# Spectral mixer block with a gated MLP: the first 512 tokens dealt out anew, so that an x tile is one transfer

## The chip, the cores and the metric

One core of one Trainium2 chip runs the whole program. The metric is the device time of one execution in microseconds (us); the median of several runs is given with the lowest and the highest. Beside the times there is one execution recorded by the hardware profiler. In its rows PE is TensorE's matmuls and PEld its weight loads, DVE is VectorE, ACT ScalarE, POOL GpSimd and SP SyncE, which only issues transfers (DMA); a name with a q behind it (SPq, ACTq) is the engine's instruction queue. L190 is line 190 of the kernel.

## The reference

x is 2048 tokens by 512 channels in float32. Cut to what matters here:

```
h = layernorm(x) * (1 + ca) + sa                       # over the channels of each token
a = h @ dft_hid_re.T ;  b = h @ dft_hid_im.T           # 512 x 512
y = dft_seq_re @ a - dft_seq_im @ b                    # 2048 x 2048, over the tokens
x = x + ga * y
h = layernorm(x) * (1 + cb) + sb
z = gelu(h @ w_in) ;  z1, z2 = halves of z ;  z2 = layernorm(z2)
out = x + gb * ((z1 * (w_sp @ z2 + b_sp)) @ w_out)     # w_sp 2048 x 2048
```

sa, ca, ga, sb, cb and gb are six rows made from a conditioning vector c. The change touches only the first sum over tokens, dft_seq times the normed x.

## The kernel before

The kernel sums over tokens first: for each output quarter t (512 rows of the DFT), for the real and the imaginary matrix j, TensorE adds up 16 products, one for each tile s of 128 tokens: the normed tile (128 tokens by 512 channels, four weight blocks of 128 channels) by T, 128 tokens by 512 DFT rows. To keep float32's precision, each operand is split into a high part (rounded to the matmul's type) and a low part (the rest), and three matmuls stand for one (`matmul3`, lines 97 to 99).

The DFT matrices lie with the output row first, so a block must be turned before it can be multiplied. A stage is 512 DFT rows by 512 tokens (`quad`), loaded by `load_block` or, in halves of 64 columns, by `load_half`: partition 32a + j holds, for 16 values of b, the row 32b + j, at 128 columns of the a-th quarter. DVE turns 32 x 32 squares (`squares`, line 190): piece k of a stage gives T with partition 32a + i holding token 128a + 32k + i. The x tile that goes with it must have the same token in the same partition, so `load_x` and `load_two` load 32 partitions at a time, four transfers for a tile or group of tiles.

The order on each engine is written by hand. The start, at the end of the function body, deals with tiles 0 to 3 (g = 0) one by one: `load_two(0)` and `load_two(1)` put each tile's four transfers on the queues of SP and ACT, two each; `load_half` brings the first half of stage 0 in between, on both queues; tiles 2 and 3, the second half of stage 0, stage 1 and tiles 4 and 5 follow on SP. `keep_busy` lets TensorE multiply ones in the meantime. `stats_first` makes a tile's statistics on DVE with two small steps on GpSimd; `whole_first` norms tile 0 on ACT, unsplit; `hi_first`, `norm_x` and `lo_h` make the high and the low part (hh, hl) of tiles 1 to 3. `turn_whole` turns the first DFT piece unsplit; `prep_hi(n)` turns piece n on DVE and makes its high part AH on ACT, `prep_lo(n)` its low part AL on DVE. The engines take these in the order of the calls: DVE's is the statistics of tile 0, pieces 0 and 1, the statistics of tile 1, AL1, the statistics of 2 and 3, hl1, pieces 2 and 3, and so on. `mm_a(n)` is TensorE's share of piece n. For n = 0 it multiplies in plain float32 (line 543, two records for each matmul), for n = 1 to 3 it takes the three products one after the other for four channel blocks (line 549), and from n = 4 on it calls `matmul3`. Its four channel blocks go in the order 1, 2, 3, 0 for n below 4.

Of the 32 stages of DFT blocks, those with g = 0 hold the first 512 tokens: stages 0 and 1 in the first quarter, then one in four.

Of the kernel before, what the change touches and what calls it, by code (L numbers as in the profile page):

```python
# [20 lines left out]
def fnet_gmlp_kernel(  # L21
# [111 lines left out]
    def quad(a, r, k):  # L133
        return a[r * Q:(r + 1) * Q, k * Q:(k + 1) * Q]

    src = []
    for t in range(NQ):
        for g, j in ([(g, j) for g in range(NQ) for j in range(2)] if t == 0 else
                     [(g, j) for j in range(2) for g in range(NQ)]):
            src.append(quad((cr, ci)[j], t, g))  # L140
    N2 = 4 * len(src)
    N1 = N2 + 8
    YPROD = (6, 7, 4, 5, 3)
# [13 lines left out]
    def load_half(tile_, a, h, engs=(nc.sync,) * 4):  # L157

        v = a.rearrange("(b j) (a s) -> a j b s", j=32, a=4)
        for q in range(4):  # L160
            engs[q].dma_start(tile_[32 * q:32 * q + 32], v[q][:, :, 64 * h:64 * h + 64])

    XB = []

    def load(b):
        if b < len(src):
            stage[b] = blocks.tile([P, 16, P], F32, tag="stage", bufs=2, name=f"stage{b}")
            load_block(stage[b], src[b])
        elif b < len(src) + 2:
            j = b - len(src)  # L170
            XB.append(blocks.tile([P, 4, Q], F32, tag="stage", bufs=2, name=f"xb{j}"))
            for g in range(2):
                nc.sync.dma_start(XB[j][:, 2 * g:2 * g + 2], ht_d[g].rearrange("(k p) t -> p k t", p=P)[:, 2 * j:2 * j + 2])
                for kk in range(2):
                    TT[2 * j + kk, g] = XB[j][:, 2 * g + kk]
        elif 4 * (b - NB0) < NE - N4:
            i, gh = divmod(b - NB0, NQ)
            g, h = divmod(gh, 2)
            p = PROD[i]
            stage[b] = blocks.tile([P, 2, 16, 64], F32, tag="stage", bufs=2, name=f"stage{b}")  # L180
            for r in range(2):
                load_half(stage[b][:, r], s_d[S_OF[p], r, g] if p in S_OF else
                          quad(w_sp, r + (2 if p == 4 else 0), g + (2 if p == 1 else 0)), h)
# [68 lines left out]
    def prep_hi(n):  # L252
        if n >= NE or n in highs:
            return
        highs.add(n)
        if N2 <= n < N4:
            T[n] = form_t(n)
        else:
            b, k = divmod(n, 4) if n < N2 else (NB0 + (n - N4) // 4, (n - N4) % 4)
            if b != NB0:  # L260
                T[n] = blocks.tile([P, Q], F32, tag="t", bufs=2, name=f"t{n}")
            if b == NB0:
                assert n in T
            elif n >= N4:
                squares(T[n], stage[b][:, k % 2], k // 2)
            else:
                squares(T[n], stage[b], k)
        AH[n] = SE[2][:, n - N4] if N4 <= n < N4 + 4 else blocks.tile([P, Q], F32R, tag="ah", bufs=4, name=f"ah{n}")
        nc.scalar.activation(AH[n], T[n], AF.Copy)  # L269
        if not N2 <= n < N4 and k == 3:  # L270
            stage.pop(b)
            if b != NB0:
                load(b + 2)
# [91 lines left out]
    def keep_busy(n, k):  # L365

        ps = bank(k, "busyp")
        for _ in range(n):
            nc.tensor.matmul(ps, ones, busy, start=True, stop=True)

    def fold_sum(t, w, u):

# [49 lines left out]
    def load_x(g, ks=range(4), eng=nc.sync):  # L422
# [1 line left out]
        if g not in XG:  # L424
            XG[g] = spool.tile([P, 4, D], F32, tag="x", bufs=2, name=f"x{g}")
        k0, k1 = ks[0], ks[-1] + 1
        v = x.rearrange("(g a k i) d -> g a i k d", g=NQ, a=4, i=32)
        for a in range(4):
            eng.dma_start(XG[g][32 * a:32 * a + 32, k0:k1, :], v[g, a][:, k0:k1, :])
        for k in ks:  # L430
            X[4 * g + k] = XG[g][:, k, :]

# [12 lines left out]
        eng.tensor_scalar(mv[:, 3:4], mv[:, 0:1], mv[:, 2:3], -1.0, op0=ALU.mult, op1=ALU.mult)  # L445
        NRM[s] = mv[:, 2:3], mv[:, 3:4]

    two = (nc.sync, nc.sync, nc.scalar, nc.scalar)

    def load_two(k):  # L450
        if not k:
            XG[0] = spool.tile([P, 4, D], F32, tag="x", bufs=2, name="x0")
        v = x.rearrange("(g a k i) d -> g a i k d", g=NQ, a=4, i=32)
        for a in range(4):
            two[a].dma_start(XG[0][32 * a:32 * a + 32, k, :], v[0, a][:, k, :])
        X[k] = XG[0][:, k, :]

    def whole_first(s):

        LN[s] = spool.tile([P, D], F32, tag="xn", bufs=4, name=f"xn{s}")  # L460
        nc.scalar.activation(LN[s].rearrange("p (k a i) -> p k a i", a=4, i=32),
                             X[s].rearrange("p (a k i) -> p k a i", a=4, i=32), AF.Identity,
                             bias=NRM[s][1], scale=NRM[s][0])
        nc.scalar.activation(LN[s][:, :1], ones[:, :1], AF.Copy)

    def split_first(s):
# [6 lines left out]

    def turn_whole(n):
        T[n] = blocks.tile([P, Q], F32, tag="t", bufs=2, name=f"t{n}")
        squares(T[n], stage[0], n)
        highs.add(n)
        lows.add(n)

# [604 lines left out]
            mm([n])  # L1084


    load_two(0)
    stage[0] = blocks.tile([P, 16, P], F32, tag="stage", bufs=2, name="stage0")
    load_half(stage[0][:, :, :64], src[0], 0, two)
    load_two(1)  # L1090
    nc.scalar.activation(sc, ones[:, :ND], AF.Silu)
    load_x(0, range(2, 4))
    load_half(stage[0][:, :, 64:], src[0], 1)
    load(1)
    load_x(1, range(2))
    keep_busy(3, 5)
    ones_x(1)
    ones_x(2)
    ones_x(3)
    stats_first(0)  # L1100
    whole_first(0)
    turn_whole(0)
    prep_hi(1)
    stats_first(1)
    prep_lo(1)
    hi_first(1)
    stats_first(2)
# [342 lines left out]
```

## Time and profile before

| | us |
|---|---|
| median of 3 runs | 931.57 |
| lowest and highest | 931.29, 931.63 |
| the profiled execution's own time | 931.77 |
| its span, first to last instruction | 930.0 |

The page of the profile gives the busy time of each engine as a share of the span; that of TensorE tells nothing of single waits, which the list of waits does (who waited for whom, and how long in all). The chain of waits follows the work that ended last back from the end; the timeline lists an engine's instructions in order of time, runs of one kind merged (x4). Times count from the first instruction.

### The profile page before, as it was taken

The numbers are of one execution on the slowest core, as the hardware profiler recorded it, in microseconds if no ns is written. First come the engines' busy times: TensorE is split into PE (matmuls) and PEld (weight loads), VectorE is DVE, ScalarE is ACT, GpSimd is POOL, SyncE is SP. The second block draws the span as 40 slices with busy tenths as digits, with TensorE's granted clock in tenths as the row PEclk, the third lists the DMA queues.
The fourth block names the chain that finished last, engine by engine and source line by source line (L and its number), as shares of the span: only waits on it lengthen the run. The fifth ranks groups of instructions, "written<-read, shape, count | busy, mean of one in ns | idle before, by whom it ended". The sixth has DMA issues, their size and how long they took to land.

```text
span 930.0 us, 12339 instructions
## 1 busy us (share of the span) xinstructions
PE 924.2 (99%) x4053; PEld 760.4 (82%) x4053; DVE 738.2 (79%) x1218; ACT 409.1 (44%) x733; POOL 199.1 (21%) x375
## 2 busy tenths in 40 slices
PE   9999999999999999999999999999999999999998
PEld 5888888888888888888888888888888888888887
DVE  7799968787687677875678788899799789986762
ACT  5694424232132222322577877674544544331121
POOL 2330000224554165323512321331000000000000
PEclk9999999999999999999999999999999999999999
DMA  9995762856639977996463864444464566734651
GB/s 218 225 227 118 142 158 46 193 147 171 158 91 319 283 220 217 275 343 227 141 217 130 279 201 103 118 105 105 105 146 102 130 142 143 178 97 149 185 178 57
DMA packets 246976, 157.88 MB, mean 170 GB/s; under 512 B 140384, under 2 KB 214368, under 8 KB 246784
## 3 DMA queue, kind: packets, MB, share of 16 engines
q1 hardware_dynamic: 233248, 119.57, 52.2%
q0 software_dynamic: 12272, 36.86, 11.4%
q8 instruction: 32, 0.52, 0.2%
q10 hardware_dynamic: 1392, 0.66, 0.2%
q14 instruction: 32, 0.26, 0.1%
HBM read 120.33 MB, written 36.71 MB: 169 GB/s over the span
## 4 chain that ended last, share of the span: by engine, by line
PE 98%; DMA 1%; SPq 0%; ACTq 0%; DVE 0%; ACT 0%; issue 0%; DVEq 0%
PE gp L99 12%; PE gp L97 12%; PE gp L98 12%; PE gw L99 10%; PE gw L97 10%; PE gw L98 10%; PE yp L99 3%; PE yp L98 3%; PE yp L97 3%; PE op L98 3%; PE op L97 3%; PE op L99 3%; PE fp L98 1%; PE fp L97 1%; PE fp L99 1%; PE z2s L98 1%
## 5 line engine op out<-in xcount | busy, mean ns | idle before, releaser
L269 ACT ACTIVATE ah<-t 128x512 fp32r<-128x512 f32 x235 | 148.5, 632 | 362.6 <-DVE t L190 242.7
L287 DVE TENSOR_TENSOR al<-t,ah 128x512 fp32r<-128x512 f32 x235 | 160.6, 683 | 55.7 <-PE gp L98 30.9
L98 PE MATMUL gp<-al,hh 128*128 128x512 f32 x496 | 193.0, 389 | 0.0
L97 PE MATMUL gp<-ah,hh 128*128 128x512 f32 x496 | 193.0, 389 | 0.0
L99 PE MATMUL gp<-ah,hl 128*128 128x512 f32 x496 | 193.0, 389 | 0.0
L190 DVE STREAM_TRANSPOSE t<-stage 128x512 f32<-128x512 f32 x236 | 165.5, 702 | 6.3 <-DMA stage<-in_A_dft_seq_re_dram 3.1
L98 PE MATMUL gw<-al,bh 128*128 128x512 f32 x400 | 155.6, 389 | 0.0
L99 PE MATMUL gw<-ah,bl 128*128 128x512 f32 x384 | 149.5, 389 | 0.0
L97 PE MATMUL gw<-ah,bh 128*128 128x512 f32 x384 | 149.4, 389 | 0.0
L98 PEld LDWEIGHTS gp<-al,hh 128*128 128x128 f32 x496 | 93.1, 188 | 19.5 <-DVE al L287 0.2
L97 PEld LDWEIGHTS gp<-ah,hh 128*128 128x128 f32 x496 | 93.1, 188 | 19.4
L99 PEld LDWEIGHTS gp<-ah,hl 128*128 128x128 f32 x496 | 93.1, 188 | 19.3
L98 PEld LDWEIGHTS gw<-al,bh 128*128 128x128 f32 x400 | 75.1, 188 | 15.7
L99 PEld LDWEIGHTS gw<-ah,bl 128*128 128x128 f32 x384 | 72.1, 188 | 15.3 <-DVE bl L948 0.3
L97 PEld LDWEIGHTS gw<-ah,bh 128*128 128x128 f32 x384 | 72.1, 188 | 14.9
L920 POOL DMA_DIRECT2D s_d<-sj x64 | 35.1, 548 | 107.2 <-DVE sj L912 82.3
L97 PE MATMUL yp<-hth,gh 128*128 128x512 f32 x128 | 49.8, 389 | 0.0
L98 PE MATMUL yp<-htl,gh 128*128 128x512 f32 x128 | 49.8, 389 | 0.0
L99 PE MATMUL yp<-hth,gl 128*128 128x512 f32 x128 | 49.8, 389 | 0.0
L665 POOL DMA_DIRECT2D ht_d<-hturn x62 | 41.0, 667 | 23.1 <-DVE hturn L661 18.2
L97 PE MATMUL op<-woh,uh 128*128 128x512 f32 x110 | 42.8, 389 | 0.0
L98 PE MATMUL op<-wol,uh 128*128 128x512 f32 x110 | 42.8, 389 | 0.0
(247 smaller groups left out, 1449.4 us busy)
## 6 DMA issues: line engine op xcount, KB each, us to landing
stage<-in_A_dft_seq_im_dram SPq DMA_DIRECT2D x64, 256.0 KB, 6.0
sj<-in_B_w_sp_dram SPq DMA_DIRECT2D x32, 512.0 KB, 7.2
s_d<-sj POOLq DMA_DIRECT2D x64, 256.0 KB, 4.7
stage<-s_d SPq DMA_DIRECT2D x128, 128.0 KB, 2.9
stage<-in_A_dft_seq_re_dram SPq DMA_DIRECT2D x60, 256.0 KB, 5.6
stage<-in_B_w_sp_dram SPq DMA_DIRECT2D x88, 128.0 KB, 3.0
wm<-in_w_mod_dram SPq DMA_DIRECT2D x16, 256.0 KB, 6.1
xr<-in_A_x_dram POOLq DMA_DIRECT2D x16, 256.0 KB, 4.5
```

Source lines behind the costliest of these rows:

```text
L97: nc.tensor.matmul(acc, ah, bh, start=first, stop=False, skip_group_check=go_on)
L98: nc.tensor.matmul(acc, ah, bl, start=False, stop=False, skip_group_check=go_on)
L99: nc.tensor.matmul(acc, al, bh, start=False, stop=last, skip_group_check=go_on)
L190: nc.vector.transpose(dst.rearrange("p (b i) -> p b i", i=32), block[:, :, 32 * k:32 * k + 32])
L269: nc.scalar.activation(AH[n], T[n], AF.Copy)
L287: nc.vector.tensor_tensor(AL[n], t, AH[n].bitcast(F32), op=ALU.subtract)
L665: eng.dma_start(v[a, i], ht[32 * a:32 * a + 32].rearrange("c (b r) -> c b r", r=32))
L920: nc.gpsimd.dma_start(s_d[m, r, g][b * P:(b + 1) * P, :], a)
```

## The change

The first 512 tokens (g = 0) are dealt out anew: tile 2h + k holds in partition p the token 256h + 2p + k. A tile is then 128 rows of x at a distance of two rows, and `load_x` brings it in one transfer on SP; the tiles of the other three groups are loaded as before. To match, a stage with g = 0 is loaded by `load_pairs` in two halves of four transfers each (partition 32a + j takes columns 256h + 64a to 256h + 64a + 63), in pieces of 64 numbers (256 bytes), where `load_block` loads pieces of 128; and `turn_dft` turns it from every second column. ACT's queue keeps two transfers at the start, those of stage 0's first half. The normed tile 0 is made in two ACT steps of two channel blocks each (1 and 2, then 0 and 3). `keep_busy` issues two matmuls of 512 columns and one of 256 where it issued three of 512. The statistics of tile 1 go ahead of `prep_hi(1)`.

```diff
--- before.py
+++ after.py
@@ -133,11 +133,12 @@
     def quad(a, r, k):
         return a[r * Q:(r + 1) * Q, k * Q:(k + 1) * Q]
 
-    src = []
+    src, SRC_G = [], []
     for t in range(NQ):
         for g, j in ([(g, j) for g in range(NQ) for j in range(2)] if t == 0 else
                      [(g, j) for j in range(2) for g in range(NQ)]):
             src.append(quad((cr, ci)[j], t, g))
+            SRC_G.append(g)
     N2 = 4 * len(src)
     N1 = N2 + 8
     YPROD = (6, 7, 4, 5, 3)
@@ -160,12 +161,30 @@
         for q in range(4):
             engs[q].dma_start(tile_[32 * q:32 * q + 32], v[q][:, :, 64 * h:64 * h + 64])
 
+    def load_pairs(tile_, a, h, engs=(nc.sync,) * 4):
+
+        v = a.rearrange("(b j) (h a s) -> h a j b s", j=32, a=4, h=2)
+        for q in range(4):
+            engs[q].dma_start(tile_[32 * q:32 * q + 32, :, 64 * h:64 * h + 64], v[h, q])
+
+    def turn_dft(n, block, k):
+
+        if SRC_G[n // 4]:
+            squares(T[n], block, k)
+        else:
+            v = block.rearrange("p b (h i c) -> p b h i c", h=2, c=2)
+            nc.vector.transpose(T[n].rearrange("p (b i) -> p b i", i=32), v[:, :, k // 2, :, k % 2])
+
     XB = []
 
     def load(b):
         if b < len(src):
             stage[b] = blocks.tile([P, 16, P], F32, tag="stage", bufs=2, name=f"stage{b}")
-            load_block(stage[b], src[b])
+            if SRC_G[b]:
+                load_block(stage[b], src[b])
+            else:
+                for h in range(2):
+                    load_pairs(stage[b], src[b], h)
         elif b < len(src) + 2:
             j = b - len(src)
             XB.append(blocks.tile([P, 4, Q], F32, tag="stage", bufs=2, name=f"xb{j}"))
@@ -264,7 +283,7 @@
             elif n >= N4:
                 squares(T[n], stage[b][:, k % 2], k // 2)
             else:
-                squares(T[n], stage[b], k)
+                turn_dft(n, stage[b], k)
         AH[n] = SE[2][:, n - N4] if N4 <= n < N4 + 4 else blocks.tile([P, Q], F32R, tag="ah", bufs=4, name=f"ah{n}")
         nc.scalar.activation(AH[n], T[n], AF.Copy)
         if not N2 <= n < N4 and k == 3:
@@ -365,8 +384,8 @@
     def keep_busy(n, k):
 
         ps = bank(k, "busyp")
-        for _ in range(n):
-            nc.tensor.matmul(ps, ones, busy, start=True, stop=True)
+        for w in n:
+            nc.tensor.matmul(ps[:, :w], ones, busy[:, :w], start=True, stop=True)
 
     def fold_sum(t, w, u):
 
@@ -424,9 +443,14 @@
         if g not in XG:
             XG[g] = spool.tile([P, 4, D], F32, tag="x", bufs=2, name=f"x{g}")
         k0, k1 = ks[0], ks[-1] + 1
-        v = x.rearrange("(g a k i) d -> g a i k d", g=NQ, a=4, i=32)
-        for a in range(4):
-            eng.dma_start(XG[g][32 * a:32 * a + 32, k0:k1, :], v[g, a][:, k0:k1, :])
+        if g:
+            v = x.rearrange("(g a k i) d -> g a i k d", g=NQ, a=4, i=32)
+            for a in range(4):
+                eng.dma_start(XG[g][32 * a:32 * a + 32, k0:k1, :], v[g, a][:, k0:k1, :])
+        else:
+            v = x.rearrange("(g h p k) d -> g h p k d", g=NQ, h=2, k=2)
+            for k in ks:
+                eng.dma_start(XG[g][:, k, :], v[0, k // 2][:, k % 2, :])
         for k in ks:
             X[4 * g + k] = XG[g][:, k, :]
 
@@ -445,22 +469,16 @@
         eng.tensor_scalar(mv[:, 3:4], mv[:, 0:1], mv[:, 2:3], -1.0, op0=ALU.mult, op1=ALU.mult)
         NRM[s] = mv[:, 2:3], mv[:, 3:4]
 
-    two = (nc.sync, nc.sync, nc.scalar, nc.scalar)
-
-    def load_two(k):
-        if not k:
-            XG[0] = spool.tile([P, 4, D], F32, tag="x", bufs=2, name="x0")
-        v = x.rearrange("(g a k i) d -> g a i k d", g=NQ, a=4, i=32)
-        for a in range(4):
-            two[a].dma_start(XG[0][32 * a:32 * a + 32, k, :], v[0, a][:, k, :])
-        X[k] = XG[0][:, k, :]
+    def halves(h, s):
+
+        v = X[s].rearrange("p (a k i) -> p k a i", a=4, i=32)
+        for ks in (slice(1, 3), slice(0, 4, 3)):
+            nc.scalar.activation(h[:, ks], v[:, ks], AF.Identity, bias=NRM[s][1], scale=NRM[s][0])
 
     def whole_first(s):
 
         LN[s] = spool.tile([P, D], F32, tag="xn", bufs=4, name=f"xn{s}")
-        nc.scalar.activation(LN[s].rearrange("p (k a i) -> p k a i", a=4, i=32),
-                             X[s].rearrange("p (a k i) -> p k a i", a=4, i=32), AF.Identity,
-                             bias=NRM[s][1], scale=NRM[s][0])
+        halves(LN[s].rearrange("p (k a i) -> p k a i", a=4, i=32), s)
         nc.scalar.activation(LN[s][:, :1], ones[:, :1], AF.Copy)
 
     def split_first(s):
@@ -473,7 +491,7 @@
 
     def turn_whole(n):
         T[n] = blocks.tile([P, Q], F32, tag="t", bufs=2, name=f"t{n}")
-        squares(T[n], stage[0], n)
+        turn_dft(n, stage[0], n)
         highs.add(n)
         lows.add(n)
 
@@ -1084,24 +1102,24 @@
             mm([n])
 
 
-    load_two(0)
+    load_x(0, range(1))
     stage[0] = blocks.tile([P, 16, P], F32, tag="stage", bufs=2, name="stage0")
-    load_half(stage[0][:, :, :64], src[0], 0, two)
-    load_two(1)
+    load_pairs(stage[0], src[0], 0, (nc.sync, nc.sync, nc.scalar, nc.scalar))
+    load_x(0, range(1, 2))
     nc.scalar.activation(sc, ones[:, :ND], AF.Silu)
     load_x(0, range(2, 4))
-    load_half(stage[0][:, :, 64:], src[0], 1)
+    load_pairs(stage[0], src[0], 1)
     load(1)
     load_x(1, range(2))
-    keep_busy(3, 5)
+    keep_busy((Q, Q, Q // 2), 5)
     ones_x(1)
     ones_x(2)
     ones_x(3)
     stats_first(0)
     whole_first(0)
     turn_whole(0)
+    stats_first(1)
     prep_hi(1)
-    stats_first(1)
     prep_lo(1)
     hi_first(1)
     stats_first(2)
```

## Rows read from the trace of the kernel before

**Rows 1.** Page, busy times: us (share of the span) x instructions

```profile
PE 924.2 (99%) x4053; PEld 760.4 (82%) x4053; DVE 738.2 (79%) x1218; ACT 409.1 (44%) x733; POOL 199.1 (21%) x375
```

**Rows 2.** Waits of TensorE, whole run: us, times, longest us

```profile
PE gp L549 <- ACT ah L269: 0.7, 1, 0.7
```

**Rows 3.** Chain of waits, 0 to 16 us: start us, us, what

```profile
8.40 4.31 DMA stage<-in_A_dft_seq_re_dram
...
12.83 0.72 DVE t L190
...
13.57 0.64 ACT ah L269
```

**Rows 4.** Timeline of TensorE, 0 to 21 us: start, us, instruction, count, idle before

```profile
1.53 5.46 PE L369 MATMUL busyp<-busy,ones 128*128 128x512 f32 x6 [1.53 <-DVE busy L308]
6.82 3.85 PE L543 MATMUL gp<-t,xn 128*128 128x512 f32 x8
10.52 1.19 PE L549 MATMUL gp<-ah,hh 128*128 128x512 f32 x4
...
14.26 1.20 PE L549 MATMUL gp<-ah,hh 128*128 128x512 f32 x4 [0.72 <-ACT ah L269]
...
20.08 0.39 PE L98 MATMUL gp<-al,hh 128*128 128x512 f32 x1
```

**Rows 5.** DMA issues near 1 and 10.5 us: KB, us to landing

```profile
x<-in_A_x_dram ACTq DMA_DIRECT2D x2, 64.0 KB, 2.3
...
stage<-in_A_dft_seq_im_dram SPq DMA_DIRECT2D x2, 256.0 KB, 6.3
```

**Rows 6.** Timeline of DVE, 0 to 21 us

```profile
3.84 0.69 DVE L439 BATCH_NORM_STATS2 first<-x 128x6 f32<-128x512 f32 x1 [2.46 <-DMA x<-in_A_x_dram]
...
5.68 0.21 DVE L445 TENSOR_SCALAR first<-first 128x1 f32<-128x1 f32 x1 [0.74 <-POOL first L443]
5.96 1.30 DVE L190 STREAM_TRANSPOSE t<-stage 128x512 f32<-128x512 f32 x2
...
9.31 0.69 DVE L439 BATCH_NORM_STATS2 first<-x 128x6 f32<-128x512 f32 x1 [0.47 <-DMA x<-in_A_x_dram]
...
11.45 0.69 DVE L525 TENSOR_TENSOR hl<-xn,hh 128x512 fp32r<-128x512 f32 x1
...
17.72 1.30 DVE L190 STREAM_TRANSPOSE t<-stage 128x512 f32<-128x512 f32 x2
19.13 0.69 DVE L287 TENSOR_TENSOR al<-t,ah 128x512 fp32r<-128x512 f32 x1
```

**Rows 7.** Timeline of ACT, 0 to 21 us

```profile
5.93 0.81 ACT L461 ACTIVATE xn<-x,first 128x512 f32<-128x512 f32 x1 [0.41 <-DVE first L445]
...
9.66 0.81 ACT L483 ACTIVATE hh<-x,first 128x512 fp32r<-128x512 f32 x1 [1.73 <-DMA stage<-in_A_dft_seq_re_dram]
```

**Rows 8.** Timeline of SP's queue: DMA issues

```profile
0.73 0.86 SPq L455 DMA_DIRECT2D x<-in_A_x_dram  x2
...
4.84 1.98 SPq L429 DMA_DIRECT2D x<-in_A_x_dram  x4
6.86 2.02 SPq L161 DMA_DIRECT2D stage<-in_A_dft_seq_re_dram  x4
8.93 3.14 SPq L155 DMA_DIRECT2D stage<-in_A_dft_seq_im_dram  x4
```

**Rows 9.** Stretches of 1 us: engines' busy time, clock, DMA share, GB/s

```profile
5.00:6.00 1.00, 1.00 (x3) 0.34 (x1) 0.25 (x2) 0.58 (x3) 0.55 (x1) 1.00 1.17 321
9.00:10.00 1.00, 1.00 (x3) 0.38 (x2) 0.69 (x1) 0.34 (x1) 0.53 (x2) 1.00 0.82 185
13.00:14.00 1.00, 0.54 (x3) 0.12 (x1) 1.00 (x2) 0.42 (x1) 0.00 (x0) 1.00 1.23 259
```

**Rows 10.** Timeline near 161 us, DVE and TensorE

```profile
160.77 0.65 DVE L287 TENSOR_TENSOR al<-t,ah 128x512 fp32r<-128x512 f32 x1
...
161.55 0.42 PE L98 MATMUL gp<-al,hh 128*128 128x512 f32 x1
```

## What the change does to the time, predicted before it ran

> **What bounds the kernel now.** I read the page's busy times first: TensorE is busy for 924.2 of the 930.0 us span [rows 1]. Then the list of TensorE's waits over the whole run. It has two lines: one of 1.5 us before the first warm-up matmul, and one of 0.7 us at L549 for AH, once [rows 2]. So after that wait TensorE never waits again for anything listed, and whatever the change does at the start shifts everything behind it by that much; elsewhere it can only lose. I call the four sequence tiles that open the kernel rows 0 to 3 (tile s with DFT row block T_s), and the next one row 4. T_s is the turned block, AH_s and AL_s its high and low halves, hh_s and hl_s those of the normed tile.
>
> The chain of waits says what the 0.7 us is: the last quarter of the second half of stage 0 is issued at 8.40 and lands 4.31 us later, at 12.71; T2 is turned from 12.83, AH2 made from 13.57 to 14.21, and row 2 starts at 14.26 [rows 3]. The timeline of TensorE gives the frame: warm-up from 1.53 for 5.46 us, row 0 at 6.82, row 1 at 10.52, row 2 at 14.26, the second matmul of row 4 (it reads AL4) at 20.08 [rows 4]. A gain is therefore the time by which row 2 starts earlier, at most, provided rows 3 and 4 follow without a gap.
>
> **How early row 0 can start.** Today x tile 0 comes in four transfers on two queues, the later pair landing 2.3 us (median) after issue [rows 5]; DVE starts on it at 3.84, ends the norm's last small step at 5.89 (5.68 + 0.21), and turns T0 from 5.96 [rows 6]. So from the start s of the statistics, T0 starts at s + 2.1 and ScalarE at s + 2.09 (5.93) [rows 6, 7].
> After the change tile 0 is one 256 KB transfer, issued first on SP. Bounds for s: not below 3.0 (a single 64 KB part issued at 0.73 lands some 2.1 to 2.3 us later), and no better than 3.84 if the whole must pass beside the two stage transfers that ScalarE's queue now issues first. I take 3.3, the nearer to the lower end, because the second pair of issues (some 0.45 us later [rows 8]) is what goes: three more quarters, 192 KB, cost 0.6 us at the 321 GB/s of 5 to 6 us, when two queues moved x rows [rows 9], and that is their price if none of it overlaps the latency of the first. Then T0 starts at A = 5.4 if stage 0's first half is there. That half is issued up to 0.9 us earlier on ScalarE's queue, where two x issues no longer stand ahead of it, so it doesn't decide. A is 0.56 earlier than 5.96.
> The normed row in two halves: the whole costs 0.81 [rows 7], a half between 0.41 and 0.81; I take 0.5, since most of it goes by the columns. The first half is done at s + 2.09 + 0.5 = 5.9, T0 at 5.4 + 0.65 = 6.05; row 0 starts at about 6.1 instead of 6.82. The second half is done at 6.4, before the third of the four matmuls wants it: it costs nothing unless matmuls are far quicker than the 0.86 us that two records of row 0 take.
>
> **What row 2 then waits for.** (a) The DMA: SP's issues ahead of stage 0's second half fall from ten to six (two for tile 0, two for stage 0, two for tile 1 and four for tiles 2 and 3 become one, two, one and two); today those of tiles 2 and 3 alone go from 4.84 to 6.82, and the half's own from 6.86 to 8.88 [rows 8]. They can now start near 3.5 and end near 5.9. The bytes ahead are the same, and 256-byte pieces alone move at 185 GB/s (9 to 10 us [rows 9]). At about 200 GB/s the 512 KB behind the x tiles take 2.6 us, from about 7.0, so it lands at 9.7 to 10.5 instead of 12.71.
> (b) Then DVE's order is late next. Behind T0 the list is now: statistics of tile 1, T1, AL1, statistics of 2 and 3, hl1, T2. With the starts of [rows 6]: statistics 1 at A + 0.65; T1 one statistics block (about 1.0) later at A + 1.6, done A + 2.3; AH1 0.63 on ScalarE, done A + 2.95; AL1 from there, and the statistics of 2 0.62 later at A + 3.6 = 9.0. Two blocks take 2.14 (9.31 to 11.45), so hl1 starts at 11.13, T2 0.62 later at 11.75, done 12.45; AH2 (0.63) done 13.12; row 2 at 13.17 against 14.26: **1.09 us earlier**. The same in differences: 0.56 (A) + 0.47 (DVE's wait for tile 2 at 9.31, gone) + 0.69 (its wait for stage 0 ahead of 12.83, gone) - 0.65 (the turn of T1 put behind the statistics, so that DVE idles while AH1 is made) = 1.07.
> (c) Is TensorE there? Row 0 works 3.70 us in 6.82 to 10.52. Starting at 6.1 at the clock it has then (below) it ends by 9.8 to 10.2. hh1 is today made at 9.66 to 10.47 [rows 7], and row 1 starts at 10.52 on it. With the statistics of tile 1 moved ahead of T1, and A, hh1 comes at about 9.3. Row 1 works 3.0 us and ends at 12.8 to 13.2. So both arrive together and about 0.05 us stays.
> (d) Row 3 and row 4. T4 starts at 17.72 and AL4 ends at 19.82, 0.26 before its matmul at 20.08 [rows 4, 6]. All that leads there follows from AH2, so it moves by the same 1.07, if stage 1 has landed by 16.6. Its last quarter today lands 6.3 us after an issue near 10.5, at about 17 [rows 5]. It now comes as eight transfers of 128 KB in 256-byte pieces: four more issues of about 0.5 on SP, with the next x load queued behind them, which nothing wants before 22 us. Started 2 to 3 us earlier and at 200 GB/s (1 MB in 5.2), it lands at 15 to 15.5: 1.1 us to spare.
>
> **Other parts.** Six more stage blocks, in later stages, get eight issues instead of four: 2 us more of SP's queue each, and the block is loaded one block ahead. By then DMA moves half of what it does at the start, so I cost these at nothing; without that cover, a block that is late costs its lateness. The 32 turned blocks with every second column: I price the turn at its 0.70, bounds 0 and +0.7 each (twice the time); the nearest row is the present turn, whose pieces of 32 elements lie apart already. The shorter warm-up takes half a matmul of the six records off TensorE, 0.85 us, and ends at about 5.8.
>
> **Sum.** 931.77 is the profiled execution's own time (span 930.0 and 1.77 around it); 931.77 - 1.07 = 930.7. The median of the runs is 0.20 lower, so **930.5 us**, a gain of 0.12%. Since 0.2% (1.86 us) is about what a measurement of this kernel can tell from no change, this is "same".
>
> **Rivals.**
> *A: tile 0 comes no earlier.* The transfer shares the engines with the stage halves from 0.73 on; s stays 3.84. Then A is 5.96 and row 2 gains 0.47 + 0.69 - 0.65 = 0.5: 931.0 to 931.1. For it: both queues now start on different things in the same microsecond; against: the two stage transfers beside it are issued at the same time, not before it. Chance 0.13.
> *B: the clock.* Warm-up records take 0.91 us, row 0's 0.48 (5.46/6, 3.85/8) [rows 4]: the first are at 1.2 GHz, the second at 2.4, and today TensorE is busy without a break from 1.53 to 10.5. Now there is a hole of about 0.3 us at 5.8. If the clock rises later for it, row 0 wholly at 1.2 GHz takes 3.4 us more and ends near 13.2, row 1 at 16.2, row 2 starts 1.9 late: 933.5. A rise at the old moment costs nothing that row 2 feels. I give 0.12 to a loss, most of it partial (931 to 932.5). The Trainium skill ("TensorE: Matmul & The Clock Gate", "What's actually happening") says that activity releases a throttle and that the moment varies from run to run; by it a hole as short as this would seldom matter, which no run here shows yet.
> *C: a turn of every second column is slower.* Then the forecast ends on the other side. T0, T1, T2 are all ahead of row 2, T3, T4, T5 ahead of AL4, and DVE has stretches without slack later: AL52 ends at 161.42, 0.13 before its matmul at 161.55 [rows 10]. With e more per turn, row 2 moves by 3e and AL4 by up to 6e; from e = 0.18 the gain is gone, and at e = 0.7 row 4 is 2 to 3 us late and the tight stretches add 4 to 5: 937. For it: no row has such a read. Chance 0.06. The Trainium skill ("SBUF — State Buffer", "Door 1: The DMA port swizzle", its note on cachelines) says that accesses run at full rate while at least two fall in the same line of 16 bytes, which a read of every second four-byte element does; by it e would be 0, and no row here shows it.
> *D: stage 1 is late.* If 256-byte pieces run worse than 185 GB/s beside other traffic (512-byte ones make 259 at 13 to 14 us [rows 9]), stage 1 lands after 16.6 and row 4 takes over as the wait, each us late costing one: landing at 17.2 leaves 0.5 of the gain, 931.1. Chance 0.07. The Trainium skill ("DMA: Bandwidth & Descriptors", "Specifications") wants 512 bytes for line rate, which speaks for this one.
> *E: it doesn't do what it says.* If T0 is held until the whole of stage 0 is in, because the strided read is taken to touch both halves, row 0 starts near 11 and row 2 near 17.4: 934.7. Chance 0.03.
> *F: more than 1.86 us.* It would need rows 0 and 1 at 2.4 GHz from 5.7 on and T2 a microsecond before DVE can reach it. Chance 0.03.
>
> **How the numbers follow.** Forecast 0.56 (own range 930.1 to 930.9), A 0.13, B 0.12, C 0.06, D 0.07, E 0.03, F 0.03. Range 929.9 to 932.2: it leaves out C, E, F and the worst third of B, 0.16. Faster by over 0.2%: F and a tail, 0.05. Slower: C, E and B's worst end, 0.10. Same: 0.85.
>
> **What would show it.** In the profile after: statistics of tile 0 at 3.3 (A: 3.84); T0's group at 0.70 a turn (C: more); no wait of T2 for stage 0; row 0 at 6.1 and records of 0.43 to 0.48 from about 7.2 on (B: 0.86 for longer); row 2 at 13.2 with at most 0.2 of wait; T4 not waiting for stage 1 (D); TensorE without any further wait. A row 2 later than 14 would make the prediction wrong.

## The result, and the profile after

| | before, us | after, us |
|---|---|---|
| median of 22 runs of each | 931.48 | 932.92 |
| lowest and highest | 931.06, 932.55 | 931.90, 934.61 |
| the profiled execution's own time | 931.77 | 933.21 |
| its span | 930.0 | 931.4 |

The change makes the kernel slower by 1.44 us: the ratio of the times is 1.0015, with a 95% interval of 1.0008 to 1.0021. The forecast was 930.5 (a gain of 1.07), its range 929.9 to 932.2: the sign was wrong, and the time lies outside the range.

Busy times are as they were [rows 1]; the list of TensorE's waits is not. Page of after (busy times), and its list of waits (us, times, longest us):

```profile
PE 924.4 (99%) x4053; PEld 761.1 (82%) x4053; DVE 738.0 (79%) x1218; ACT 408.8 (44%) x734; POOL 200.5 (22%) x375
```

```profile
PE gp L561 <- DVE t L176: 2.2, 1, 2.2
PE busyp L388 <- DVE busy L327: 1.5, 1, 1.5
```

The one wait on AH2 [rows 2] has gone, and a wait three times as long stands in another place: row 0 (now L561) waits for T0. The chain of waits and the timeline of TensorE, 0 to 22 us of after (start us, us, what):

```profile
1.65 5.45 DMA stage<-in_A_dft_seq_re_dram
...
7.21 0.72 DVE t L176
...
8.07 5.37 PE gp L561 x8
13.44 2.75 PE gp L567 x12
```

```profile
1.53 4.38 PE L388 MATMUL busyp<-busy,ones 128*128 128x512 f32 x6 [1.53 <-DVE busy L327]
8.07 5.37 PE L561 MATMUL gp<-t,xn 128*128 128x512 f32 x8 [2.16 <-DVE t L176]
12.88 1.48 PE L567 MATMUL gp<-ah,hh 128*128 128x512 f32 x4
...
16.02 1.07 PE L567 MATMUL gp<-ah,hh 128*128 128x512 f32 x4
...
21.69 0.39 PE L98 MATMUL gp<-al,hh 128*128 128x512 f32 x1
```

Against [rows 4]: the warm-up ends 1.1 us earlier as meant, row 0 starts 1.25 later, takes 4.81 us to the start of row 1 where it took 3.70, and row 2 starts at 16.02 instead of 14.26, **1.76 later**: 1.25 (T0 at 7.21, was 5.96) + 1.11 (row 0) + 0.12 (row 1) - 0.72 (the old wait). The second matmul of row 4 is 1.61 late and the whole 1.44. From there on nothing changes: the own time less the start of row 4 is 911.8 after and 911.9 before, and between 911.6 and 912.2 in every kernel below. The six other stages that are loaded in narrower pieces cost nothing that shows beside this scatter.

T0 is late because two things that it needs are late, and they come within 0.1 us of each other. The chain goes by stage 0's first half: a transfer of it, issued at 1.65, lands 5.45 later, at 7.10, where in before T0 found the half there at 5.96 [rows 6]. And DVE ends tile 0's norm at 7.13 (6.92 + 0.21). Either alone would have held T0 to about 7.2. The timeline of DVE and of SP's queue, after:

```profile
5.08 0.69 DVE L463 BATCH_NORM_STATS2 first<-x 128x6 f32<-128x512 f32 x1 [3.69 <-DMA x<-in_A_x_dram]
...
6.92 0.21 DVE L469 TENSOR_SCALAR first<-first 128x1 f32<-128x1 f32 x1 [0.74 <-POOL first L467]
7.21 0.71 DVE L176 STREAM_TRANSPOSE t<-stage 128x512 f32<-128x512 f32 x1
7.85 0.65 DVE L463 BATCH_NORM_STATS2 first<-x 128x6 f32<-128x512 f32 x1
...
8.82 0.70 DVE L176 STREAM_TRANSPOSE t<-stage 128x512 f32<-128x512 f32 x1
...
10.83 0.69 DVE L463 BATCH_NORM_STATS2 first<-x 128x6 f32<-128x512 f32 x1
...
12.85 0.68 DVE L543 TENSOR_TENSOR hl<-xn,hh 128x512 fp32r<-128x512 f32 x1
13.45 1.30 DVE L176 STREAM_TRANSPOSE t<-stage 128x512 f32<-128x512 f32 x2
...
18.33 1.30 DVE L176 STREAM_TRANSPOSE t<-stage 128x512 f32<-128x512 f32 x2
```

```profile
0.73 0.39 SPq L453 DMA_DIRECT2D x<-in_A_x_dram  x1
1.17 0.95 SPq L168 DMA_DIRECT2D stage<-in_A_dft_seq_re_dram  x2
2.17 1.44 SPq L453 DMA_DIRECT2D x<-in_A_x_dram  x3
5.41 1.92 SPq L168 DMA_DIRECT2D stage<-in_A_dft_seq_re_dram  x4
```

The statistics of tile 0 start at 5.08 where they started at 3.84 [rows 6], though only one transfer is issued for it, at the same 0.73. The issues of 0.6 to 0.9 us and of 6.8 to 7.1 us (KB, us to landing) show it: 4.3 us to landing, not the 2.3 of the quarters before [rows 5], beside a stage transfer that ACT's queue issues in the same moment.

```profile
x<-in_A_x_dram SPq DMA_DIRECT2D x1, 256.0 KB, 4.3
stage<-in_A_dft_seq_re_dram ACTq DMA_DIRECT2D x1, 128.0 KB, 4.7
...
stage<-in_A_dft_seq_re_dram SPq DMA_DIRECT2D x1, 128.0 KB, 5.0
```

And row 0 is slow because of TensorE's clock. Stretches of after (busy us and count of PE, PEld, DVE, ACT, POOL; granted clock; DMA share; GB/s):

```profile
1.50:5.50 4.00, 3.97 (x5) 1.85 (x6) 0.42 (x1) 1.49 (x2) 0.00 (x0) 1.00 0.99 210
5.60:8.90 3.30, 1.14 (x4) 0.49 (x3) 2.34 (x9) 1.30 (x3) 0.55 (x1) 1.00 1.14 282
9.00:12.30 3.30, 3.30 (x5) 1.35 (x4) 2.54 (x6) 2.24 (x4) 1.11 (x3) 0.50 1.10 215
12.40:20.00 7.60, 7.60 (x33) 5.95 (x32) 6.43 (x13) 5.93 (x11) 2.90 (x5) 1.00 1.14 230
```

TensorE was busy up to 5.9 and again from 8.07, for 1.14 of the 3.30 us from 5.6 to 8.9; from 9.0 to 12.3 it is granted 0.50, that is 1.2 GHz instead of 2.4, while it works without a break. Row 0's weight loads stand 0.85 us apart there, and 0.43 apart behind 12.4. The 1.00 of the first stretch is no measurement: the trace's record of the clock begins at 5.55, and up to about there the warm-up's matmuls stand 0.85 apart as well. So the clock was up from 5.55 to 8.97, and down from there to 12.38.

### The profile page after: what moved, and what is told of

The parts are those of the page before. It is cut to its first block, busy times and chain, and to the rows that moved or that the text cites. A ratio compares the mean times of both kernels' runs of the same rounds, so it can differ in the third digit from the quotient of the medians.

```text
span 931.4 us, 12366 instructions
## 1 busy us (share of the span) xinstructions
PE 924.4 (99%) x4053; PEld 761.1 (82%) x4053; DVE 738.0 (79%) x1218; ACT 408.8 (44%) x734; POOL 200.5 (22%) x375
## 4 chain that ended last, share of the span: by engine, by line
PE 99%; DMA 1%; DVE 0%; SPq 0%; issue 0%; DVEq 0%
PE gp L99 12%; PE gp L97 12%; PE gp L98 12%; PE gw L99 10%; PE gw L98 10%; PE gw L97 10%; PE yp L99 3%; PE yp L97 3%; PE yp L98 3%; PE op L99 3%; PE op L97 3%; PE op L98 3%; PE fp L97 1%; PE fp L99 1%; PE fp L98 1%; PE z2s L99 1%
## 5 line engine op out<-in xcount | busy, mean ns | idle before, releaser
L209 DVE STREAM_TRANSPOSE t<-stage 128x512 f32<-128x512 f32 x204 | 143.4, 703 | 5.6 <-DMA stage<-in_B_w_sp_dram 1.7
```

What stands on the lines that cost most here:

```text
L209: nc.vector.transpose(dst.rearrange("p (b i) -> p b i", i=32), block[:, :, 32 * k:32 * k + 32])
```

## The experiments

Own times of kernels come beside runs of the kernel before on the same chip. Each kernel goes by the first part of its name (e2, b1). In nearly all of them one reading carries the argument: the start of T2 on DVE. Row 2 starts 1.42 or 1.43 us behind T2 in before and in thirteen of the fourteen kernels below; in after and in e4_contig it starts 2.57 behind it, and both show row 0 at 5.37 us and the low clock. (e9_sp4 shows that clock too, but there T2 is so late that row 2 still waits for it.) So T2 tells how late the data are, and what stands above 1.43 is the clock.

**The clock.** Two theories for the 1.44 us: the hole in TensorE's work lets the clock fall (called K), or all of it is late data (D). A longer warm-up closes the hole and leaves the data as they are.

```diff
-    keep_busy((Q, Q, Q // 2), 5)
+    keep_busy((Q, Q, Q, Q, Q // 2), 5)     # e2_warm45
+    keep_busy((Q, Q, Q), 5)                # e1_warm3
```

> The changed kernel with four and a half warm-up matmuls instead of two and a half; nothing else. Theory K (clock): in the changed kernel TensorE idles from about 5.9 us to 8.07, the granted clock falls at 8.97 and comes back at 12.38, and row 0 takes 4.8 us instead of 3.7. Without the hole the clock stays up once it has risen; row 0 (start near 8.1 to 8.6) takes at most 3.7, row 1 begins by 12.2, and row 2 is bound by AH2 at about 14.85 (0.6 later than before): about 0.6 us slower than the kernel before, and the spread between runs shrinks. Theory D (data alone: row 0's late start explains all): as slow as the changed kernel, 1.4 us over before.

Measured: 931.94 (931.83 to 932.23), before 931.26 there, ratio 1.0008 (0.9999 to 1.0018). Timeline of TensorE, e2:

```profile
1.53 7.01 PE L388 MATMUL busyp<-busy,ones 128*128 128x512 f32 x10 [1.53 <-DVE busy L327]
8.38 3.60 PE L561 MATMUL gp<-t,xn 128*128 128x512 f32 x8
11.41 1.49 PE L567 MATMUL gp<-ah,hh 128*128 128x512 f32 x4
...
14.66 1.20 PE L567 MATMUL gp<-ah,hh 128*128 128x512 f32 x4
```

Row 0 starts 0.31 later than in after and row 1 1.47 earlier; granted clock 1.00 from 7.6 on. So K holds: about half of the loss goes by giving TensorE more to do, and the highest of e2's ten runs lies below 17 of after's 22. The other half stays: T2 is at 13.24, little better than after's 13.45.

> The changed kernel with the warm-up of before (three matmuls): the hole ahead of row 0 shrinks from about 2.2 us to between 1.1 and 1.8. Theory K (clock): fewer executions lose the clock, so the time lies between that of the run with four and a half matmuls (0.7 us over before) and the changed kernel (1.4 to 1.5 over), at about 0.8 to 1.2 over before. If the hole as such doesn't matter and only the number of warm-up matmuls does, it is at 0.7.

Measured: 932.33 (931.78 to 933.38), ratio 1.0011 (1.0002 to 1.0020). As K forecast, the time lies between e2 and after. The hole is 1.4 us in the profiled execution, which shows no fall, and the runs divide by the granted clock that each of them lists: four at 0.998 (932.79 to 933.38), six at 0.999 or 1.000 (931.78 to 932.57). The same division goes through after itself: ten of its 22 runs list 0.997 or 0.998, with a median of 932.99, and of the twelve at 1.000 the lowest six lie at 931.90 to 932.34, where e2 is. None of the 85 runs of before beside the experiments lists less than 0.999. So a fall costs about 1.0 us (1.15 in the trace, 2.57 less 1.42) and comes in nearly half of after's runs. The medians of the ten and of the twelve, 932.99 and 932.52, are only 0.5 apart, because the other six of the twelve took 932.70 to 934.61 with no fall listed; what they lost is left open.

Does any hole cost? The kernel before with the shorter warm-up alone:

```diff
-        for _ in range(n):
-            nc.tensor.matmul(ps, ones, busy, start=True, stop=True)
+        for w in n:
+            nc.tensor.matmul(ps[:, :w], ones, busy[:, :w], start=True, stop=True)
...
-    keep_busy(3, 5)
+    keep_busy((Q, Q, Q // 2), 5)
```

> The kernel before with the changed kernel's warm-up (two and a half matmuls): the hole in TensorE's work is about 0.9 us, from 5.9 to 6.8, instead of 2.2. Theory K (clock): the hole can let the granted clock fall or rise later, in some executions and not in others: time 0 to 1 us over before with a wider spread. Rival (only a long hole matters, and row 2 waits for stage 0 anyway): no difference, and the same spread as before.

Measured: 931.48 (930.90 to 932.27) against 931.33, ratio 1.0002 (0.9993 to 1.0012). Waits of TensorE:

```profile
PE gp L543 <- ACT xn L464: 0.9, 1, 0.9
```

A hole of 0.9 us here, none of ten runs below 0.999: no loss. The shorter warm-up does no harm by itself; it does when T0 comes late on top of it. In the profiled executions of all kernels the clock fell behind holes of 1.88 (e4), 2.16 (after) and 2.55 us (e9), and not behind any of 1.44 (e1) or less.

**Why tile 0 is late.** Theories: the one wide transfer for 128 partitions is the slow thing (called W); its company is (the stage transfer on the other queue in the same microsecond, C); or the spacing of its rows, which now lie 4 KB apart in x where they were neighbours (S). First the width undone, tile 0 in four parts on both queues as before, ahead of the stage (e3):

```diff
-    load_x(0, range(1))
+    XG[0] = spool.tile([P, 4, D], F32, tag="x", bufs=2, name="x0")
+    for i, eng in enumerate((nc.sync, nc.sync, nc.scalar, nc.scalar)):
+        eng.dma_start(XG[0][32 * i:32 * i + 32, 0, :],
+                      x.rearrange("(g h p k) d -> g h p k d", g=NQ, h=2, k=2)[0, 0][32 * i:32 * i + 32, 0, :])
+    X[0] = XG[0][:, 0, :]
```

> The changed kernel, but tile 0 comes in four transfers of 32 partitions again, two on SP and two on ACT, ahead of the stage transfers on both queues; the new deal of tokens (rows 4 KB apart) and everything else stay. Theory C (company): tile 0 was late (statistics at 5.08 instead of 3.84) because ACT's stage transfers start in the same microsecond; then here the statistics start at 3.8 to 4.0 and row 0 near 6.7. Theory S (spacing): rows 4 KB apart are slow to fetch; then the statistics stay at 4.6 or later. Theory W (one wide transfer): as C, 3.8 to 4.0.

Measured: 932.41 (931.68 to 934.40), ratio 1.0015 (1.0005 to 1.0025). Timeline of DVE, e3:

```profile
3.91 0.69 DVE L463 BATCH_NORM_STATS2 first<-x 128x6 f32<-128x512 f32 x1 [2.52 <-DMA x<-in_A_x_dram]
...
5.93 0.71 DVE L176 STREAM_TRANSPOSE t<-stage 128x512 f32<-128x512 f32 x1
7.41 0.70 DVE L463 BATCH_NORM_STATS2 first<-x 128x6 f32<-128x512 f32 x1 [0.77 <-DMA x<-in_A_x_dram]
```

Tile 0 is back at 3.9, as C and W forecast, and the stage's first half comes with it: T0 starts at 5.93 without a wait. Yet the median gains nothing that can be told from after: tile 1, still one transfer, now makes DVE wait 0.77 us, and T2 is at 13.05. (The profiled execution, 931.68, is the fastest of the ten; what the median lost beyond it no trace shows.)

The row spacing undone (e4): tiles 0 to 3 from 128 neighbouring rows each.

```diff
-                eng.dma_start(XG[g][:, k, :], v[0, k // 2][:, k % 2, :])
+                eng.dma_start(XG[g][:, k, :], x[P * k:P * k + P, :])
```

> The changed kernel, but each of tiles 0 to 3 loads 128 neighbouring rows of x in one transfer, so that the tokens of these tiles don't match the DFT blocks; the work is the same otherwise. Theory S (spacing): the statistics of tile 0 start at 3.3 to 3.8. Theories C and W: they stay at about 5.1, because the company and the single transfer are unchanged.

Measured: 931.71 (931.34 to 933.41), ratio 1.0007 (0.9998 to 1.0017); statistics at 4.58, T2 at 13.05, and the low clock in the profiled execution (row 0 5.37), the only one of ten that lists a fall. 4.58 lies between the two forecasts: if the spacing tells, it isn't all. By the median this edit gives back more than any other single one: of 1.44 us over before, 0.45 are left, and the interval takes in no loss at all.

The company undone (e5): all of the stage's first half on SP, behind tile 0.

```diff
-    load_pairs(stage[0], src[0], 0, (nc.sync, nc.sync, nc.scalar, nc.scalar))
+    load_pairs(stage[0], src[0], 0)
```

> The changed kernel, but all four transfers of stage 0's first half are issued on SP behind tile 0, and ACT issues none. Theory C (company): tile 0 has the engines to itself, statistics at 3.3 to 3.6; the stage half lands later than 7.1 by up to 1 us or at the same time. Theories S and W: statistics of tile 0 still near 5.

Measured: 932.83 (932.05 to 933.35), ratio 1.0016 (1.0007 to 1.0026); statistics at 4.32, between the forecasts again. Tile 0 gains 0.4 to 0.8 us, and tile 1, now behind four stage transfers, takes it back: its statistics wait 1.03 us until 8.23 (7.85 in after), and T2 is at 13.87. The same kernel again (f2), and both edits, of e4 and of e5, together (f1):

> The changed kernel with all four transfers of stage 0's first half on SP behind tile 0, a second look at the same kernel: statistics of tile 0 at 4.32 again within 0.2, so that the difference to the run with neighbouring rows can be read; if it is off by more, that difference can't be.

> The changed kernel with all four transfers of stage 0's first half on SP behind tile 0, so that tile 0 is alone, and with tiles 0 to 3 loaded from 128 neighbouring rows each (their tokens then don't match the DFT blocks). If the width alone makes tile 0 late: statistics at 4.2 to 4.4, as alone with rows 4 KB apart (4.32). If the spacing of the rows does: 3.3 to 3.8.

Measured: f2 932.39 and f1 931.11, single runs, before 931.32. Timeline of DVE, f1, then f2:

```profile
3.52 0.69 DVE L463 BATCH_NORM_STATS2 first<-x 128x6 f32<-128x512 f32 x1 [2.13 <-DMA x<-in_A_x_dram]
...
6.12 0.71 DVE L176 STREAM_TRANSPOSE t<-stage 128x512 f32<-128x512 f32 x1 [0.55 <-DMA stage<-in_A_dft_seq_re_dram]
```

```profile
4.03 0.69 DVE L463 BATCH_NORM_STATS2 first<-x 128x6 f32<-128x512 f32 x1 [2.65 <-DMA x<-in_A_x_dram]
```

In f1 one wide transfer of neighbouring rows, with the stage only behind it, is as early as the four narrow ones of before; but T0 gains nothing by it, for it waits 0.55 us for the stage's first half. f2 was to repeat e5's 4.32 within 0.2 for f1 to be compared with it, and came 0.29 off. So the 0.5 and 0.8 us between f1 and these two suggest a price of the spacing and don't show it: it is one execution against two, and tile 0 moves by 0.27 among four executions with the loads of before and by 0.33 among three with those of after. The company made from narrow transfers is the counter-test (e9): tile 0 in four transfers, all on SP, while ACT's queue starts the stage at 0.72; `load_two(k, cuts, engs)`, here and below, brings tile k in as many transfers as cuts says.

```diff
-    load_x(0, range(1))
+    load_two(0, 4, (nc.sync,) * 4)        # four 32-partition transfers, all issued by SP
```

> The changed kernel, but tile 0 in four transfers of 32 partitions, all on SP, while ACT issues its two stage transfers from 0.72 as in the changed kernel: narrow, with company. Theory W: the last part, issued near 2.1, lands near 4.4, statistics at 4.4 to 4.6, earlier than in the changed kernel though three issues more stand ahead; stage 0's first half is issued 1.35 later on SP and still lands near 7. Theory C (company): as late as in the changed kernel or later, 5.1 to 6.

Measured: 934.22 (933.57 to 935.05), ratio 1.0032 (1.0021 to 1.0043). Timeline of DVE and waits of TensorE, e9:

```profile
5.21 0.69 DVE L463 BATCH_NORM_STATS2 first<-x 128x6 f32<-128x512 f32 x1 [3.83 <-DMA x<-in_A_x_dram]
```

```profile
PE gp L570 <- DVE t L176: 2.6, 1, 2.6
```

Narrow transfers in that company are later still, as C forecast; but SP issues the last of them near 2.1, some 1.4 us behind the wide one of after, so 5.21 isn't the price of the company alone. Tile 0's statistics, all together:

| tile 0 | stage only behind it | a stage transfer beside it, on the other queue |
|---|---|---|
| wide, neighbouring rows | 3.52 | 4.58 |
| wide, rows 4 KB apart | 4.03, 4.32 | 4.75, 4.84, 5.08 |
| four parts on two queues, neighbouring rows (before, b0 to b2) | 3.57 to 3.84 | |
| four parts on two queues, rows 4 KB apart (e3, e6, e7) | 3.74 to 3.91 | |
| two halves on two queues, rows 4 KB apart (e8, below) | 4.12 | |
| four parts on SP, rows 4 KB apart | | 5.21 |

Company costs the wide form 0.4 to 1.1 us, the spacing of the rows 0.2 to 0.8 in the wide form and at most 0.3 in the narrow one, each from single executions that scatter by about 0.3. The width costs nothing with neighbouring rows; with spaced ones four parts are 0.1 to 0.6 earlier than one transfer, and two halves are not. In the wide form with spaced rows, 7 to 17 of tile 0's first 128 packets (2 KB each) took over 300 ns; with neighbouring rows one (e4) or none (f1) did. But slow packets by themselves don't make tile 0 late: in four parts before and e3 have none, e7 and e6 six and seven, and b1, with neighbouring rows and its tile 0 at 3.57, nine. Whether and why spaced rows hold up a wide transfer is left open.

The Trainium skill ("DMA: Bandwidth & Descriptors", "Rules for kernel authors") advises one 128-partition transfer over two to disjoint partition halves, since both share the same engines. e8 has such halves, and tile 0 is there at 4.12, where one transfer with the stage only behind it brings it at 4.03 and 4.32: the measurement agrees, halves gain nothing. What loses in after is that the stage starts beside the one transfer on the other queue, 4.75 to 5.08. Its section "Issuing engines are not separate DMA queues", which says that transfers of different queues interleave on the same engines, agrees with the price of the company.

**What is left of the change with this repaired.** Tiles 0 and 1 in four parts on both queues, three whole warm-up matmuls; once with the order of after (e6), once with T1 ahead of the statistics of tile 1 as before (e7), and once in two parts of 64 partitions (e8):

```diff
-    load_x(0, range(1))
+    load_two(0, 4, (nc.sync, nc.sync, nc.scalar, nc.scalar))     # e8: (0, 2, (nc.sync, nc.scalar))
...
-    load_x(0, range(1, 2))
+    load_two(1, 4, (nc.sync, nc.sync, nc.scalar, nc.scalar))     # e8: (1, 2, (nc.sync, nc.scalar))
...
-    keep_busy((Q, Q, Q // 2), 5)
+    keep_busy((Q, Q, Q), 5)
...
-    stats_first(1)                                               # e7 alone: behind prep_hi(1)
```

> The changed kernel, but tiles 0 and 1 each come in four transfers of 32 partitions, two on SP and two on ACT, as before the change (with the new deal of tokens), and the warm-up has three whole matmuls as before. Theory W (the wide transfer is what loses): statistics of tile 0 at 3.85, of tile 1 near 6.7 as soon as it lands; T1 near 7.6, AL1 ends 9.6, T2 near 12.3 on DVE's order, row 2 near 13.7 instead of 14.26, clock risen once and not fallen: 0.5 us faster than before. If row 2 is at 14.2 or later with tiles 0 and 1 in time, the rest of the prediction's DVE sum is wrong too.

> As the run with tiles 0 and 1 in four transfers and three warm-up matmuls, but T1 is turned ahead of the statistics of tile 1 again. What the swap of these two is worth by itself: by the prediction's differences (0.65 lost on DVE because it idles while AH1 is made) T2 starts 0.4 to 0.65 earlier than with the swap, near 11.8, unless stage 0's second half lands later than that; row 2 near 13.3, 0.9 us faster than before. By the rival, that hh1 at the head of row 1 is what counts, row 1 starts later than with the swap and TensorE loses it.

> As the run with tiles 0 and 1 in four transfers and three warm-up matmuls (swap kept), but each of the two tiles in two transfers of 64 partitions, one on SP and one on ACT, so that tile 0 is out after one issue on each queue. If issues are what tile 0 waits for: statistics at 3.3 to 3.5, 0.4 earlier than with four transfers. If the width of a transfer is what costs (theory W): 3.9 or later, between four parts (3.91) and one (4.3 alone, 5.1 in company).

Measured, before 931.23: e6 931.43 (931.28 to 931.52), ratio 1.0001 (0.9991 to 1.0010); e7 931.27 (930.88 to 931.52), 0.9998 (0.9989 to 1.0007); e8 931.85 (931.55 to 931.99), 1.0006 (0.9997 to 1.0015). Row 2 starts at 13.91, 13.74 and 14.57. Timeline of DVE, e6, then e7:

```profile
3.74 0.69 DVE L463 BATCH_NORM_STATS2 first<-x 128x6 f32<-128x512 f32 x1 [2.36 <-DMA x<-in_A_x_dram]
...
6.03 0.71 DVE L176 STREAM_TRANSPOSE t<-stage 128x512 f32<-128x512 f32 x1 [0.23 <-DMA stage<-in_A_dft_seq_re_dram]
```

```profile
11.70 0.69 DVE L552 TENSOR_TENSOR hl<-xn,hh 128x512 fp32r<-128x512 f32 x1 [0.59 <-ACT xn L121]
12.31 1.30 DVE L176 STREAM_TRANSPOSE t<-stage 128x512 f32<-128x512 f32 x2
```

With the loads repaired the loss is gone, and there is no gain either: tile 0 is early, but T0 waits 0.23 us for stage 0's first half in e6 and 0.39 in e7 (until 6.21). The swap of the order is worth less than it was priced at: with the old order the statistics of tile 2 start at 9.02 instead of 9.88, but hl1 then waits 0.59 for the normed tile 1, and T2 comes 0.18 earlier, not 0.65. In e8 tile 0 is at 4.12 and not at 3.3 to 3.5, so it isn't issues that it waits for, and T0 waits 0.74 for the stage. The swap alone, in the kernel before (b2), and the kernel before once more (b0):

```diff
-    prep_hi(1)
     stats_first(1)
+    prep_hi(1)
     prep_lo(1)
```

> The kernel before with the statistics of tile 1 put ahead of T1, alone. By the prediction's step for DVE: hl1 is made 0.65 later (about 11.6 to 12.3), row 1 starts earlier (about 10.2), and T2 waits for stage 0's second half as before, so row 2 stays near 14.2: no difference. If T2 comes to start later than the half lands, up to 0.4 us slower.

> The kernel before, unchanged, for a second look at its start: how far tile 0's statistics (3.84), stage 0's second half (landed 12.71) and row 2 (14.26) move from one execution to the next. If the profile of before was a usual one, all three within 0.2 us; if not, part of what is read as gained or lost against it is chance.

Measured: b2 931.50 (931.43 to 932.74) against 931.33, ratio 1.0003 (0.9994 to 1.0013), T2 at 12.72, no difference, as forecast; b0 931.62 in its single run. Timeline of TensorE, b0, then of DVE, b1:

```profile
13.97 1.21 PE L549 MATMUL gp<-ah,hh 128*128 128x512 f32 x4 [0.40 <-ACT ah L269]
```

```profile
5.88 1.30 DVE L190 STREAM_TRANSPOSE t<-stage 128x512 f32<-128x512 f32 x2 [0.25 <-DMA stage<-in_A_dft_seq_re_dram]
```

The wait that the change was to remove was 0.72 in the execution on which the prediction rests [rows 2] and is 0.40 here, nothing in b1 (row 2 at 13.40): from one execution to the next row 2 moved by 0.29 and more, where within 0.2 was expected. And T0, which found its stage half there in that execution, waits for it in all three others with the old loads: 0.18 us in b0 (T0 at 5.95), 0.25 in b1 (5.88), 0.62 in b2 (6.27). None of these kernels is measurably faster than before.

## Why the prediction was wrong

**The first step that failed: s, the start of tile 0's statistics.** It was put at 3.3, with bounds of 3.0 and 3.84; measured are 5.08, 4.84 and 4.75. The value fits a wide transfer of neighbouring rows with the stage only behind it (3.52), which is not what the change issues. The upper bound was no bound: "no better than 3.84 if the whole must pass beside the two stage transfers" says how good it can be in that case, and was used as how bad. The argument against rival A, that the stage transfers are issued at the same time and not before, was the error itself: at the same time is what costs 0.4 to 1.1. And that the rows of a tile now lie 4 KB apart stood in the diff and got no price.

**The second, beside it: the stage half that "doesn't decide".** It was put at nothing because it is issued up to 0.9 us earlier. It landed at 7.10, and the chain of after goes by it: with that landing T0 would have come at about 7.2, and not at 5.4, however early tile 0 was. Why the half landed so late has no run of its own; in e3, where only the transfers of tile 0 are others, it is there by 5.93. It decides elsewhere as well: T0 waits for it in b0, b1 and b2, in e6 and e7, and in f1, where tile 0 is at 3.52. No kernel here has T0 before 5.88, so the 0.56 us that the sum takes from A was not to be had by an earlier tile 0. In e6 the sum holds from T0 on (T2 6.46 behind it, 6.35 put), and 0.63 of the 0.74 us by which row 2, at 13.91, misses 13.17 is T0 at 6.03.

**The step that failed by these two: the hole.** Put at 0.3 us, it was 2.2: the warm-up ended at 5.9, close to the 5.8 that was put, and row 0 started at 8.07 and not at 6.1. Rival B thereby came near the mechanism, but its chance of 0.12 was that of a short hole, and it was priced as a clock that rises late; what the trace shows is a clock that had risen and fell behind the hole. That B's full price, row 2 1.9 us late, is near the measured 1.76 is luck: it has row 0 at the low clock from end to end and no late T0 in it. The Trainium skill ("TensorE: Matmul & The Clock Gate", "What's actually happening"), by which activity releases a throttle and the moment varies from run to run, was used for a loss that seldom matters. The traces agree with it in both points, 0.50 behind the idle stretch, and three warm-up matmuls that take from 4.28 us (b2) to 5.46 (before) as the clock rises earlier or later; with the hole at its real size the loss came in ten of 22 runs.

**The sum of the two.** Row 2 was put at 13.17 and started at 16.02. Of these 2.85 us, T2 at 13.45 instead of 11.75 is 1.70, and row 2 starting 2.57 behind T2 instead of 1.42 is 1.15. The profiled execution's own time shows 2.51 of it (933.21 against 930.7): from row 2 to the second matmul of row 4 it takes 5.67 us and not 5.82 [rows 4], and the rest is scatter behind that. Against before, the median's 1.44 is some 0.7 for late data, which e2 keeps, and some 0.7 that goes when the hole is closed; the clock's fall accounts for that in the ten runs that list it, and in the other slow ones it isn't shown. The forecast called the change "same", within 1.86 us, and 1.44 is within it; but the sign was the other one, so that was luck.

**What held.** (b) DVE's order: from T0 to T2 it was 6.35, measured 6.24 (7.21 to 13.45), and statistics 1, T1 and statistics 2 stand 0.64, 1.61 and 3.62 behind T0 where 0.65, 1.6 and 3.6 were put. C, the turn of every second column, did not come true. Groups by line of after (count, us, mean ns, then idle before):

```profile
L209 DVE STREAM_TRANSPOSE t<-stage 128x512 f32<-128x512 f32 x204 | 143.4, 703 | 5.6 <-DMA stage<-in_B_w_sp_dram 1.7 <-DMA stage<-in_A_dft_seq_re_dram 1.3 <-DVE hl L543 0.8
L176 DVE STREAM_TRANSPOSE t<-stage 128x512 f32<-128x512 f32 x32 | 22.3, 700 | 0.2
```

700 ns each against 703 for the plain turn: e is 0. The Trainium skill's note on cachelines ("SBUF — State Buffer", "Door 1: The DMA port swizzle") gave this, and the trace agrees. D didn't come either: T4 is turned at 18.33 without a wait, stage 1 having landed at 16.1, before the 16.6 that was wanted, with the range 15 to 15.5 missed by 0.6 to 1.1. E didn't: T0 runs long before the second half of stage 0 is in.

**What was wrong without mattering.** (a) The second half of stage 0 was put at 9.7 to 10.5 and landed at 11.8: the last quarter, issued at 6.84, took 5.0 us, and SP's queue stood still from 3.6 to 5.4 (a wait of 1.8 us for a stage transfer, in its list of waits) so that its issues began at 5.41 and not near 3.5. T2 didn't wait for it. (c) hh1 began at 10.10 and not 9.3, and TensorE was later still. The two halves of the normed row were right to cost nothing, 1.09 us for both against 0.81; they bring nothing either, since row 0 waits for T0. The swap (priced at 0.65, measured 0.18) and DVE's two waits (0.47 + 0.69) were read from one execution: run again, the wait for stage 0 was 0.39 instead of 0.69, and row 2 started at 13.97 instead of 14.26, so 0.3 us of the gain was in that execution alone; in b1, with the old loads as well, it started at 13.40, which leaves 0.23 of the 1.09.

## What to carry to other kernels

Ask of the first transfer of a kernel what else is issued in its microsecond, on whichever queue, and where its rows lie; a count of transfers or bytes says little about when it lands. Where a start needs two inputs, price both: an early tile gained nothing here as long as the stage half wasn't there. When a warm-up is cut to fit an earlier start, work out the hole for the late end of that start's range too, for a warm-up that ends early is harmless by 0.9 us and was not by 2.2. A gain that consists of waits of a few tenths of a microsecond should be read from two executions before it is put in a sum.

## What the runs showed of the hardware

- A 256 KB load of 128 rows of 2 KB lands 2.8 us after issue when only transfers of its own queue follow it and its rows are neighbours, 3.3 and 3.6 with rows 4 KB apart; with a stage transfer started on the other queue in the same microsecond it is 3.8 and 4.0 to 4.3 (all as the first transfer on SP's queue: f1, f2 and e5, e4, and e1, e2 and after, one execution each).
- The granted clock, at full from 5.55 us on, fell to 0.50 at 8.97 behind an idle stretch of 2.2 us although TensorE was at work again by then, and row 0 took 1.1 us more. Of runs of one and the same kernel only some show it.
- A 32 x 32 turn of float32 that reads every second element takes the same 0.70 us as one that reads neighbours.
